# Full-width value operands, load-gated weights, a split spread and a new instruction order in a gated-recurrence + MLP kernel

## The chip, the cores and the metric

The kernel runs on one core of one Trainium2 chip. The metric is the time of one execution on the device in microseconds, from repeated runs; the median of three runs of the kernel before is 234.4 us (233.44 to 235.23).

The core has five engines with a queue of instructions each, worked off in order: TensorE (PE in the profile, with its weight loads shown apart as PEld), VectorE (DVE), ScalarE (ACT), GpSimd (POOL) and SyncE (SP). Here SP only issues transfers. An engine that waits holds up everything behind it in its own queue.

## What is computed

Two layers. The first is a gated linear recurrence per batch (4) and head (8), over 768 steps, with 48 features a head; the second is an MLP from 384 to 2048 and back, with a periodic activation.

```python
f = 1.0 / (1.0 + np.exp(-f_logit))
for t in range(S):
    state = f[:, :, t, :, None] * state + np.einsum('bhd,bhe->bhde', k[:, :, t], v[:, :, t])
    y[:, :, t] = np.einsum('bhd,bhde->bhe', q[:, :, t], state)
...
h = x @ w_in                    # x: y as (3072 tokens, 384)
s = np.sin(alpha * h)
g = h + s * s / (alpha + 1e-09)
out = g @ w_out
```

Inputs and output are float32 in HBM; the kernel computes its matmuls in bf16.

## The kernel before

**Tiling.** The 768 steps are cut into 6 chunks of 128. A *unit* u is one chunk and two of the four batches, so there are 12 units, and each has four loads of 384 KB (f, k, q, v; three buffers of each). Per unit, ScalarE computes the log gate (Exp, Ln), TensorE sums it over the steps with a triangular mask ("cs"), and ScalarE exponentiates the sums with both signs ("Gi" and "G"). k is multiplied by one and q by the other into a bf16 tile "qk", and v is copied into a bf16 tile "vb".

**Attend, per chunk and batch.** The 8 heads are handled as 4 pairs, head r * 4 + p standing in half r of pair p, 64 columns each of which 48 are used. k and q are transposed (on TensorE for the first four chunks, by transfers for the last two); scores "aps" are made per pair and half (64 rows of the array); VectorE multiplies them by the causal mask into "at", one tile for each half r; and the output "y" (128 rows of features, 4 pairs, 128 steps) is gathered in PSUM from the old state (`inter_`, L424, 128 x 128 stationary) and from the chunk itself (`intra_`, L437). In `intra_` the stationary operand is the 64 columns of one head's values, and the result goes to the 64 rows of half r, so TensorE works there with a 128*64 tile. In chunk 0 there is no state, and pair 1 is spread over three blocks at once from a second tile "v1". Last, `kv_` and `st_` make the new state.

**Spread.** y is copied to xT (bf16, features by tokens). The MLP needs 384 features in 3 blocks of 128; the three pairs p = 0, 2, 3 fill them with gaps of 16, and pair 1 is moved into the gaps by six small transfers (`spread`, L488), in every chunk but the first, where `intra_` writes there at once.

**MLP, per chunk.** For each of 16 feature blocks: 3 matmuls give h (512 tokens; in chunk 0 twice 256 tokens, a tile for each pair of batches), ScalarE takes the sine (L514), POOL, VectorE or ScalarE squares it (L522, L520), VectorE adds into g (L527); then 16 matmuls for each batch give the output o (L546), which is copied and stored. ScalarE's sine and its exponentials need different tables, so each change between them is a table load of about 1.3 us.

**The order.** The functions only describe operations: the engines an operation may run on with the cost on each, what it depends on, which buffers it takes. A list scheduler (`in_order`) simulates the five engines and emits the operation that can start earliest by these costs; ties go to the lower rank, and an operation with a choice of engines compares its start on each plus that engine's BIAS. Loads, h, cs and the ScalarE operations that use a table keep given orders (LOADS, PHASES). PSUM for the recurrence is a ring of three buffers "a", shared by cs, transposes, scores, y and kv. On the chip only the order on each engine and the real dependencies hold, not the planned times.

**Weights.** w_in comes in two halves of eight transfers, w_out in four, all issued by POOL. They depend on nothing. `W_AFTER` holds times (15, 22 and 52 us) before which the planner does not place them; it fixes their place in POOL's order and nothing else.

Of the kernel before, what the change touches and what calls it, by code (L numbers as in the profile page):

```python
# [51 lines left out]
LATENCY = {"PE": 260, "ACT": 120, "DVE": 120, "POOL": 150, "SP": 0}  # L52
# [76 lines left out]
def kernel(  # L129
# [20 lines left out]
    nc = tc.nc  # L150
# [55 lines left out]
    v1_b = [consts.tile([C, 2, 2, 3 * E], BF16, name=f"v1{i}") for i in range(2)]  # L206
    v_b = [consts.tile([C, 2, 2, HP, E], BF16, name=f"vb{i}") for i in range(NV)]
# [21 lines left out]
    for i in range(max(NQ, NV)):  # L229
        for ts in (lf_b, v_b, v1_b, qk_b):  # L230
            if i >= len(ts):
                continue
            if ts is v_b:
                nc.vector.memset(ts[i][:, :, :, 0:2, D:], 0.0)
                nc.vector.memset(ts[i][:, :, :, 2:4, 0:16], 0.0)
            elif ts is v1_b:
                nc.vector.memset(ts[i], 0.0)
            else:
                nc.vector.memset(ts[i].rearrange("c x y r e -> c (x y r) e")[:, :, D:], 0.0)
# [5 lines left out]
    def load(u, n, rank):  # L245
# [9 lines left out]
        load_order.append(o)  # L255
# [6 lines left out]
    al_r = consts.tile([P, FB], F32)  # L262
    w_in_dma, w_out_dma = {0: [], 1: []}, {}
# [10 lines left out]
    def w_out_load(rank):  # L274
        src = moe_w_out.rearrange("(fb p) m -> p fb m", p=P)
        for g4 in range(4):
            def emit(e, gs=slice(4 * g4, 4 * g4 + 4)):
                nc.gpsimd.dma_start(out=w_out_bf[:, gs, :], in_=src[:, gs, :])
            w_out_dma[g4] = op(rank + 0.1 * g4, {POOL: 780}, emit, dma=2500)
            w_out_dma[g4].after = W_AFTER[2]  # L280

# [18 lines left out]
    def pre(u, rank):  # L300
        fb_, kb_, qb_, vb_ = (bufs[n, u] for n in "fkqv")
# [10 lines left out]
        def values(e):  # L312
            vi = tl["v", u].rearrange("c (b r p) d -> c (b r) p d", r=2, p=HP)
            vo = v_b[bufs["vb", u].place % NV].rearrange("c b r p e -> c (b r) p e")
            nc.vector.tensor_copy(vo[:, :, 0:2, :D], vi[:, :, 0:2, :])
            nc.vector.tensor_copy(vo[:, :, 2:4, 16:], vi[:, :, 2:4, :])
            if u < NU:
                v1 = v1_b[u].rearrange("c b r x -> c (b r) x")
                nc.vector.tensor_copy(v1[:, :, D:D + 32], vi[:, :, 1, :32])
                nc.vector.tensor_copy(v1[:, :, 2 * E:2 * E + 16], vi[:, :, 1, 32:])  # L320

        x = op(rank, {ACT: 850}, exp_, deps=[fb_.ready], holds=[fb_], table=EXP)
        l = op(rank, {ACT: 850}, ln_, deps=[x], takes=[lf], holds=[fb_], table=EXP)
        act = [x, l]
        made["v", u] = op(rank + 2, {DVE: 1000 if u < NU else 950}, values, deps=[vb_.ready], takes=[vv], holds=[vb_])
        late = []
        for i in range(2):
# [34 lines left out]
            c_ = op(rank + i, {PE: 170 if last else 420}, cs_, deps=[l], takes=[cb], holds=[lf])  # L362
            c_.line = "cs"
            cs_order.append(c_)
            gi = op(rank, {ACT: 450}, Gi_, deps=[c_], takes=[Gib], holds=[cb], table=EXP)
            g = op(rank, {ACT: 450}, G_, deps=[c_], holds=[cb], table=EXP)
# [3 lines left out]
            made["kh", m] = op(rank + i, MULS, km, deps=[gi, kb_.ready], takes=[qkb], holds=[kb_, Gib])  # L370
            made["qh", m] = op(rank + i, {DVE: 600}, qm, deps=[g, qb_.ready], takes=[qkb], holds=[qb_, cb])
            if not last:
                made["gl", m] = op(rank + i, {DVE: 160}, gl_, deps=[g], takes=[glb], holds=[cb])
        return act, late

    def pres(us, rank):
        parts = [pre(u, r) for u, r in zip(us, rank)]
        for i in range(len(parts) + 1):
            act_order.extend(parts[i][0] if i < len(parts) else [])
            act_order.extend(parts[i - 1][1] if i else [])  # L380
# [257 lines left out]
```

## Time and profile before

| | |
|---|---|
| median of three runs | 234.4 us |
| the profiled execution | 234.14 us |
| its span, first to last instruction | 232.4 us |
| TensorE busy | 193.7 us (83%) |
| VectorE busy | 167.4 us (72%) |
| ScalarE busy | 149.0 us (64%) |
| POOL busy | 121.2 us (52%) |
| read from HBM, written | 25.17 MB, 4.72 MB |
| chain of waits that ended last | TensorE 49%, VectorE 13%, transfers 13%, SP's queue 7%, POOL 6% |

How to read it: a row of the timeline has the start in us, the length in us, the engine, the line of the kernel, the operation, the tile of the array for TensorE, output and inputs, and the count of instructions merged into the row; in square brackets stand the idle time before it and what ended that. TensorE's matmuls are pipelined, and the profile models their ends, so two rows may overlap and a busy time holds more than the array's own work. The row of forty digits cuts the span into slices of 5.8 us and gives the busy tenths of each. A row of a group (`L546 PE MATMUL ...`) gives count, busy us, mean ns, and the idle time just before its instructions.

### The profile page before, as it was taken

The numbers are of one execution on the slowest core, as the hardware profiler recorded it, in microseconds if no ns is written. First come the engines' busy times: TensorE is split into PE (matmuls) and PEld (weight loads), VectorE is DVE, ScalarE is ACT, GpSimd is POOL, SyncE is SP. The second block draws the span as 40 slices with busy tenths as digits, with TensorE's granted clock in tenths as the row PEclk, the third lists the DMA queues.
The fourth block names the chain that finished last, engine by engine and source line by source line (L and its number), as shares of the span: only waits on it lengthen the run. The fifth ranks groups of instructions, "written<-read, shape, count | busy, mean of one in ns | idle before, by whom it ended". The sixth has DMA issues, their size and how long they took to land.

```text
span 232.4 us, 4292 instructions
## 1 busy us (share of the span) xinstructions
PE 193.7 (83%) x1529; PEld 111.8 (48%) x1529; DVE 167.4 (72%) x319; ACT 149.0 (64%) x239; POOL 121.2 (52%) x148
## 2 busy tenths in 40 slices
PE   0441587787769999987999999999979999799993
PEld 0330464655546655543555545544535454355552
DVE  4533548997956998988788998986845987477631
ACT  4640178988939985489899557767757555365500
POOL 5560341674832757635735644555335467588810
PEclk9999999799999999999999999999999999999999
DMA  7999999986890799973999944700049101010011
GB/s 154 212 190 211 208 209 219 222 146 91 144 174 7 142 188 227 190 185 85 192 249 184 208 71 115 171 0 3 35 112 189 36 1 39 14 68 34 34 71 68
DMA packets 115125, 29.61 MB, mean 127 GB/s; under 512 B 108720, under 2 KB 114336, under 8 KB 115104
## 3 DMA queue, kind: packets, MB, share of 16 engines
q1 hardware_dynamic: 111936, 26.19, 55.8%
q0 software_dynamic: 3168, 3.16, 8.4%
q8 instruction: 12, 0.20, 0.4%
q14 instruction: 9, 0.07, 0.1%
HBM read 25.17 MB, written 4.72 MB: 129 GB/s over the span
## 4 chain that ended last, share of the span: by engine, by line
PE 49%; DVE 13%; DMA 13%; SPq 7%; POOL 6%; issue 5%; ACT 5%; POOLq 0%; ACTq 0%
PE h L509 19%; PE o L546 18%; DMA v<-in_v_dram 6%; PE y L437 6%; DVE g L527 5%; SPq L488 4%; SPq L251 4%; POOL s L522 3%; DVE at L419 3%; DMA w_out_bf<-in_moe_w_out_dram 3%; DMA xT<-xT 2%; POOL qk L358 2%; PE aps L416 2%; DMA w_in_bf<-in_moe_w_in_dram 2%; ACT Gi L349 1%
## 5 line engine op out<-in xcount | busy, mean ns | idle before, releaser
L522 POOL TENSOR_TENSOR s<-s 128x512 f32<-128x512 f32 (+1 forms) x94 | 87.8, 944 | 63.5 <-ACT s L514 51.3
L514 ACT ACTIVATE s<-h,al_p 128x512 f32<-128x512 f32 (+1 forms) x112 | 67.6, 626 | 43.4 <-PE h L509 40.6
L527 DVE SCALAR_TENSOR_TENSOR g<-s,al_r,h 128x512 bf16<-128x512 f32 (+1 forms) x112 | 72.4, 664 | 19.1 <-POOL s L522 18.4
L509 PE MATMUL h<-xT,w_in_bf 128*128 128x512 bf16 (+1 forms) x336 | 78.5, 355 | 6.8 <-DMA xT<-xT 3.6
L546 PE MATMUL o<-w_out_bf,g 128*128 128x384 bf16 x384 | 78.5, 327 | 2.8 <-DMA w_out_bf<-in_moe_w_out_dram 1.9
L509 PEld LDWEIGHTS <-w_in_bf 128*128 128x128 bf16 x336 | 31.8, 99 | 33.0 <-issue 6.5
L546 PEld LDWEIGHTS <-g 128*128 128x128 bf16 x384 | 34.4, 97 | 27.6 <-issue 3.1
L358 POOL TENSOR_TENSOR qk<-k,Gi 128x384 bf16<-128x384 f32 x19 | 19.0, 1017 | 33.8 <-ACT Gi L349 27.1
L419 DVE TENSOR_TENSOR at<-aps,mask 128x512 bf16<-128x512 f32 x48 | 31.7, 682 | 1.4 <-PE aps L416 1.4
L437 PE MATMUL y<-at,vb 128*64 128x128 bf16 x184 | 19.6, 233 | 6.3 <-DVE at L419 5.7
L358 DVE TENSOR_TENSOR qk<-q,cs 128x384 bf16<-128x384 f32 x24 | 12.9, 546 | 8.1 <-ACT cs L345 4.1
L437 PEld LDWEIGHTS <-vb 128*64 128x64 bf16 x184 | 12.2, 114 | 13.5 <-issue 9.6
L606 ACT ACT_TABLE_LOAD x13 | 16.7, 1283 | 0.2
L458 DVE TENSOR_TENSOR st<-kv,gl 128x512 bf16<-128x512 f32 x20 | 13.7, 685 | 4.0 <-PE kv L452 4.0
L444 ACT CAST xT<-y 128x512 bf16<-128x512 f32 (+1 forms) x12 | 6.7, 562 | 14.8 <-PE y L437 14.6
L416 PE MATMUL aps<-tr 64*128 64x128 bf16 x192 | 10.8, 225 | 6.3 <-DVE qk L358 5.6
L399 PE MATMUL tp<-ident,qk 128*128 128x128 bf16 x128 | 11.5, 236 | 4.4 <-DVE al_p L290 2.4
L349 ACT ACTIVATE Gi<-cs 128x384 f32<-128x384 f32 x24 | 11.7, 486 | 4.2 <-PE cs L336 2.7
L336 PE MATMUL cs<-lf,mask 128*128 128x384 bf16 x24 | 8.1, 355 | 7.3 <-ACT lf L309 6.5
L554 DVE COPY osb<-o 128x384 f32<-128x384 f32 x14 | 7.7, 555 | 7.7 <-PE o L546 6.7
L399 PEld LDWEIGHTS <-qk 128*128 128x128 bf16 x128 | 9.2, 106 | 6.7 <-POOL qk L358 4.2
L416 PEld LDWEIGHTS <-tr 64*128 64x128 bf16 x192 | 6.0, 96 | 12.4 <-DVE qk L358 6.6
(53 smaller groups left out, 164.4 us busy)
## 6 DMA issues: line engine op xcount, KB each, us to landing
f<-in_f_logit_dram SPq DMA_DIRECT2D x12, 384.0 KB, 5.6
k<-in_k_dram SPq DMA_DIRECT2D x12, 384.0 KB, 5.4
q<-in_q_dram SPq DMA_DIRECT2D x12, 384.0 KB, 5.8
v<-in_v_dram SPq DMA_DIRECT2D x12, 384.0 KB, 6.2
out_dram<-osb SPq DMA_DIRECT2D x24, 192.0 KB, 2.1
w_out_bf<-in_moe_w_out_dram POOLq DMA_DIRECT2D x4, 384.0 KB, 6.5
w_in_bf<-in_moe_w_in_dram POOLq DMA_DIRECT2D x8, 128.0 KB, 5.6
xT<-xT SPq DMA_DIRECT2D x30, 16.0 KB, 1.8
```

The source lines that it names most:

```text
L349: nc.scalar.activation(out=tl["Gi", m], in_=tl["cs", m][:, :H * D], func=Act.Exp)
L358: engine[e].tensor_mul(qk_b[bufs["qk", m].place % NQ][:, "kq".index(n), :, :, :D], tl[n, u][:, i * H:(i + 1) * H, :].rearrange("c (r p) d ...
L399: nc.tensor.transpose(tl[x, "tp"][:, j * HP + p, :], qk_b[qkb.place % NQ][:, j, p, :, :].rearrange("c r e -> c (r e)"), ident)
L416: nc.tensor.matmul(aps[r][:, p, :], t[halves[r], p, :], t[halves[r], HP + p, :], start=True, stop=True)
L419: nc.vector.tensor_mul(tl[x, "at", r], tl[x, "a"][r], mask4)
L437: nc.tensor.matmul(tl[x, "y"][halves[r], blk, :], v_, tl[x, "at", r][:, p, :], start=(first and p == 0), stop=True, skip_group_check=True)
L509: nc.tensor.matmul(h[:, :n], w_in_bf[:, kb, fs], xT[:, kb, ts], start=(kb == 0), stop=(kb == KB - 1))
L514: nc.scalar.activation(out=s[:, :n], in_=tl[x, "h"][:, :n], func=Act.Sin, scale=al_p[:, fb:fb + 1])
L522: engine[e].tensor_mul(s2[:, :n], s[:, :n], s[:, :n])
L527: nc.vector.scalar_tensor_tensor(tl["g", c, fb][:, ts], tl[x, "s2"][:, :n], al_r[:, fb:fb + 1], tl[x, "h"][:, :n], Alu.mult, Alu.add)
L546: nc.tensor.matmul(tl["o", c, t], tl["g", c, fb][:, t * P:(t + 1) * P], w_out_bf[:, fb, :], start=(fb == 0), stop=(fb == FB - 1))
L606: nc.scalar.preload_act_table_set(now)
```

## The change

1. **Full-width values.** The tile vb gets, behind each head's 64 columns, 64 columns of zeros, so that `intra_` can take 128 columns: values and zeros for half 0, zeros and values for half 1. Each matmul now writes all 128 rows of y and adds zeros in the other half. v1 is laid out in seven fields with zeros between for the same purpose. The tiles are cleared whole at the start.
2. **Weight transfers gated by loads.** Ahead of each half of w_in and of w_out stands a one-element copy on POOL from a loaded tile: the second, the seventh and the sixteenth load of the list. The weight transfers come behind it in POOL's order.
3. **Spread in two halves.** The six transfers become two operations of three, each of which may go to SP or to POOL.
4. **A new order.** Other load order, phases (5 groups of sines instead of 7), ranks, biases and costs, and a rank offset for each kind of operation in each chunk (KIND).

```diff
-SPARE = 25
-LOADS = [("f", 0), ("f", 1), ("k", 0), ("q", 0), ("v", 0), ("q", 1), ("v", 1), ("k", 1), ("f", 2), ("k", 3), ("q", 2), ("k", 2), ("k", 4), ("f", 3), ("f", 5), ("v", 3), ("v", 2), ("q", 4), ("q", 3), ("f", 4), ("k", 5), ("q", 5), ("k", 6), ("v", 4), ("q", 6), ("v", 5), ("v", 6), ("v", 7), ("k", 7), ("f", 7), ("f", 6), ("q", 8), ("q", 7), ("f", 8), ("v", 8), ("k", 8), ("f", 9), ("k", 9), ("q", 9), ("v", 9), ("f", 10), ("k", 10), ("q", 10), ("v", 10), ("f", 11), ("k", 11), ("q", 11), ("v", 11)]
-W_AFTER = [15000, 22000, 52000]
-LAG = [50, 24, 32, 29, 28, 94]
-ATT = [-32, 18, 8, 12, -4, 16]
-PHASES = [("pre", [0]), ("pre", [1]), ("sin", 6), ("pre", [2]), ("sin", 16), ("pre", [3]), ("sin", 9),
-          ("pre", [4, 5]), ("sin", 16), ("pre", [6, 7]), ("sin", 4), ("pre", [8, 9]), ("sin", 29), ("pre",
-          [10, 11]), ("sin", 32)]
-RANK = [-100, 150, -190, 19, 50, -161, -104, -88, -100, -12, -96, -264]
-MULS = {"POOL": 1180, "DVE": 1000}
-BIAS = {"ACT": 100, "DVE": 100, "POOL": -200}
+SPARE = 15
+LOADS = [("k", 0), ("f", 0), ("q", 0), ("v", 0), ("f", 1), ("v", 1), ("q", 1), ("k", 1), ("f", 3),
+    ("k", 3), ("f", 2), ("q", 3), ("q", 2), ("f", 5), ("v", 3), ("v", 2), ("k", 2), ("k", 4),
...
+W_GATE = [1, 6, 15]
+LAG = [389, 183, 51, 210, 208, 289]
+ATT = [150, -130, -181, 58, -47, 55]
+PHASES = [("pre", [0]), ("pre", [1]), ("sin", 16), ("pre", [2, 3]), ("sin", 15), ("pre", [4, 5]),
+    ("sin", 17), ("pre", [6, 7, 8]), ("sin", 18), ("pre", [9, 10, 11]), ("sin", 46)]
+RANK = [-6, 628, -691, -10, 175, 71, 8, 20, -437, -18, -103, -123]
+MULS = {"POOL": 1020, "DVE": 750}
+KIND = {"v": [147, 9, 46, 75, 127, -2],
+        "cs": [-145, -32, -204, -182, -55, -258],
...
+SPREAD = {"SP": 1800, "POOL": 1600}
+BIAS = {"ACT": 400, "DVE": 500, "POOL": 500, "SP": -1800}
...
-    v1_b = [consts.tile([C, 2, 2, 3 * E], BF16, name=f"v1{i}") for i in range(2)]
-    v_b = [consts.tile([C, 2, 2, HP, E], BF16, name=f"vb{i}") for i in range(NV)]
+    v1_b = [consts.tile([C, 2, 2, 7, E], BF16, name=f"v1{i}") for i in range(2)]
+    v_b = [consts.tile([C, HP, 2, 2, 2, E], BF16, name=f"vb{i}") for i in range(NV)]
...
-                nc.vector.memset(ts[i][:, :, :, 0:2, D:], 0.0)
-                nc.vector.memset(ts[i][:, :, :, 2:4, 0:16], 0.0)
+                nc.vector.memset(ts[i], 0.0)
...
+    def weights_after(i, rank):
+        u, n = LOADS[W_GATE[i]][1], LOADS[W_GATE[i]][0]
+        return op(rank, {POOL: 100}, lambda e: nc.gpsimd.tensor_copy(seen[:, i:i + 1], tl[n, u][0:1, 0, 0:1]),
+                  deps=[bufs[n, u].ready], holds=[bufs[n, u]])
+
     def w_in_load(hf, rank):
+        gate = weights_after(hf, rank)
...
-                w_in_dma[hf].append(o := op(rank, {POOL: 550}, emit, dma=830 if n == E else 620 if n == D else 210))
-                o.after = W_AFTER[hf]
+                w_in_dma[hf].append(op(rank, {POOL: 550}, emit, deps=[gate],
+                                       dma=830 if n == E else 620 if n == D else 210))
...
-            vo = v_b[bufs["vb", u].place % NV].rearrange("c b r p e -> c (b r) p e")
-            nc.vector.tensor_copy(vo[:, :, 0:2, :D], vi[:, :, 0:2, :])
-            nc.vector.tensor_copy(vo[:, :, 2:4, 16:], vi[:, :, 2:4, :])
+            vo = v_b[bufs["vb", u].place % NV].rearrange("c p b r x e -> c p (b r) x e")
+            nc.vector.tensor_copy(vo[:, 0:2, :, 0, :D], vi[:, 0:2])
+            nc.vector.tensor_copy(vo[:, 2:4, :, 0, 16:], vi[:, 2:4])
...
                 if first and p == 1:
-                    v1 = v1_b[u][:, i, r, :]
-                    vs = ((0, v1[:, 0:E]), (2, v1[:, E:2 * E]), (1, v1[:, 2 * E:]))
+                    v1 = v1_b[u][:, i, r].rearrange("c x e -> c (x e)")
+                    vs = [(blk, v1[:, (2 * n + 1 - r) * E:(2 * n + 3 - r) * E]) for n, blk in enumerate((0, 2, 1))]
                 else:
-                    vs = ((POS[p], v_b[vb.place % NV][:, i, r, p, :]),)
+                    vs = [(POS[p], v_b[vb.place % NV][:, p, i].rearrange("c r x e -> c (r x e)")[:, r * E:(r + 2) * E])]
                 for blk, v_ in vs:
-                    nc.tensor.matmul(tl[x, "y"][halves[r], blk, :], v_, tl[x, "at", r][:, p, :],
-                                     start=(first and p == 0), stop=True, skip_group_check=True)
+                    nc.tensor.matmul(tl[x, "y"][:, blk, :], v_, tl[x, "at", r][:, p, :],
+                                     start=(first and p == r == 0), stop=(r == 1), skip_group_check=True)
...
-        def emit(e):
+        def emit(e, r):
             xT = tl["xT", c]
-            for r in range(2):
-                for blk, dst, src in ((0, D, 0), (2, 0, 16), (1, 0, 32)):
-                    engine[e].dma_start(out=xT[r * E + dst:r * E + dst + 16, blk, :],
-                                        in_=xT[r * E + src:r * E + src + 16, 3, :])
-        made["x", c] = op(rank, {SP: 3000}, emit, deps=[made["y", c, b] for b in range(B)],
-                          holds=[bufs["xT", c]], dma=300)
+            for blk, dst, src in ((0, D, 0), (2, 0, 16), (1, 0, 32)):
+                engine[e].dma_start(out=xT[r * E + dst:r * E + dst + 16, blk, :],
+                                    in_=xT[r * E + src:r * E + src + 16, 3, :])
+        made["x", c] = [op(rank, SPREAD, lambda e, r=r: emit(e, r), deps=[made["y", c, b] for b in range(B)],
+                           holds=[bufs["xT", c]], dma=150) for r in range(2)]
...
-        t = op(rank, {POOL: 700 if half else 1040, ACT: 420 if half else 630, DVE: 350 if half else 620}, sq, deps=[s], takes=[s2b], holds=[sb])
+        t = op(rank + KIND["sq"][c], {POOL: 640 if half else 1040, ACT: 420 if half else 640, DVE: 520 if half else 917}, sq, deps=[s], takes=[s2b], holds=[sb])
```

More of the change, by code (lines that the diff above doesn't have):

```diff
@@ L49, in __init__ @@
         self.line = table and "table"
-LATENCY = {"PE": 260, "ACT": 120, "DVE": 120, "POOL": 150, "SP": 0}
+LATENCY = {"PE": 260, "ACT": 160, "DVE": 180, "POOL": 180, "SP": 0}
 TABLE_LOAD, DMA_LATENCY, DMA_AHEAD = 1280, 1400, 1000
@@ L278, in emit @@
                 nc.gpsimd.dma_start(out=w_out_bf[:, gs, :], in_=src[:, gs, :])
-            w_out_dma[g4] = op(rank + 0.1 * g4, {POOL: 780}, emit, dma=2500)
-            w_out_dma[g4].after = W_AFTER[2]
+            w_out_dma[g4] = op(rank + 0.1 * g4, {POOL: 780}, emit, deps=[gate], dma=2500)
     def alpha(rank):
@@ L465, in attend @@
+            tr = op(rank + KIND["tr"][c], {DVE: 640, ACT: 970}, tr_, deps=[qt], takes=[trb], holds=[tpb])
         else:
             tr = op(rank, {SP: 1300}, tr_, deps=[made["kh", m], made["qh", m]], takes=[trb], holds=[qkb], dma=3000)
-        a = op(rank, {PE: 450}, a_, deps=[tr], takes=ab + atb, holds=[trb])
-        ms = [op(rank, {DVE: 690}, lambda e, r=r: m_(e, r), deps=[a], holds=[ab[r], atb[r]]) for r in range(2)]
+        a = op(rank + KIND["a"][c], {PE: 400}, a_, deps=[tr], takes=ab + atb, holds=[trb])
@@ L528, in add @@
                                            tl[x, "h"][:, :n], Alu.mult, Alu.add)
-        a = op(rank, {PE: 330 if half else 645}, mm, deps=needs, takes=[hb], holds=[bufs["xT", c]])
+        a = op(rank + KIND["h"][c], {PE: 340 if half else 655}, mm, deps=needs, takes=[hb], holds=[bufs["xT", c]])
         a.line = "h"
@@ L533, in first @@
         h_order.append(a)
-        s = op(rank, {ACT: 470 if half else 600}, sin_, deps=[a, made["al"]], takes=[sb], holds=[hb], table=TRIG)
-        t = op(rank, {POOL: 700 if half else 1040, ACT: 420 if half else 630, DVE: 350 if half else 620}, sq, deps=[s], takes=[s2b], holds=[sb])
-        made["g", c, fb, ts.start] = op(rank, {DVE: 410 if half else 690}, add, deps=[t], takes=[gb], holds=[s2b, hb])
+        s = op(rank, {ACT: 455 if half else 645}, sin_, deps=[a, made["al"]], takes=[sb], holds=[hb], table=TRIG)
+        t = op(rank + KIND["sq"][c], {POOL: 640 if half else 1040, ACT: 420 if half else 640, DVE: 520 if half else 917}, sq, deps=[s], takes=[s2b], holds=[sb])
+        made["g", c, fb, ts.start] = op(rank + KIND["g"][c], {DVE: 420 if half else 685}, add, deps=[t], takes=[gb], holds=[s2b, hb])
         return s
@@ L557, in store @@
             nc.sync.dma_start(out=out[t * S + c * C:t * S + (c + 1) * C, :], in_=tl["osb", c, t])
-        v_ = op(rank, {DVE: 550, ACT: 650}, ev, deps=[prev], takes=[sbuf], holds=[ob])
+        v_ = op(rank + KIND["ev"][c], {DVE: 520, ACT: 500}, ev, deps=[prev], takes=[sbuf], holds=[ob])
         op(rank, {SP: 500}, store, deps=[v_], holds=[sbuf], dma=700)
@@ L566 @@
     made["al"] = alpha(EARLY)
+    for u in range(NCH * NU):
+        for n in "fkqv":
+            load(u, n, EARLY)
+    load_order += [bufs[x].ready for x in LOADS]
     w_in_load(0, EARLY)
```

103 lines of the change are left out of this document (56 added, 47 removed), and 4 rows, old and new, of the table LOADS.

## The prediction

> **What bounds the kernel now.** I read the forty slices of the page first, then the stretches, then TensorE's instructions in order of time, then the waits.
>
> ```profile
> span 232.4 us, 4292 instructions
> PE   0441587787769999987999999999979999799993
> DVE  4533548997956998988788998986845987477631
> DMA  7999999986890799973999944700049101010011
> GB/s 154 212 190 211 208 209 219 222 146 91 144 174 7 142 188 227 190 185 85 192 249 184 208 71 115 171 0 3 35 112 189 36 1 39 14 68 34 34 71 68
> 0.00:72.00 72.00, 43.29 (x421) 30.97 (x422) 46.61 (x117) 44.41 (x77) 34.13 (x64) 0.98 0.99 176
> 72.00:220.00 148.00, 142.03 (x1062) 76.10 (x1061) 117.42 (x197) 103.54 (x162) 85.41 (x83) 1.00 0.52 109
> ```
>
> The stretch rows give, after the length, the busy us of PE, PEld, DVE, ACT and POOL, then clock, DMA share and GB/s. There are two regimes. From 72 to 220 us TensorE is busy 142.03 of 148: what shortens its work there shortens the kernel, as long as VectorE (117.42, four fifths of the stretch) follows. Up to 72 us TensorE is busy 43.29 of 72 and waits for others, while the DMA slices stand at 9 tenths for some 46 us. The profiled execution took 234.14 us, 1.7 more than its span and next to the median of 234.4; I work from 234.1.
>
> **Part 1, the padded values.** A TensorE busy time contains the modelled end of each matmul, so I measure from start to start.
>
> ```profile
> 182.96 0.82 PE L509 MATMUL h<-xT,w_in_bf 128*128 128x512 bf16 x3
> 183.62 0.39 PE L424 MATMUL y<-tr,st 128*128 128x128 bf16 x4
> 183.84 0.33 PE L546 MATMUL o<-w_out_bf,g 128*128 128x384 bf16 x1
> ...
> 187.24 0.81 PE L509 MATMUL h<-xT,w_in_bf 128*128 128x512 bf16 x3
> 187.98 0.41 PE L437 MATMUL y<-at,vb 128*64 128x128 bf16 x4
> 188.32 0.50 PE L546 MATMUL o<-w_out_bf,g 128*128 128x384 bf16 x2
> ...
> 55.89 0.42 PE L437 MATMUL y<-at,vb 128*64 128x128 bf16 x8
> 56.24 0.39 PE L450 MATMUL kv<-st,ident 128*128 128x512 bf16 x1
> ...
> 72.00:220.00 148.00, 12.96 (x132) 7.89 (x130) 1.00 0.52 109
> ```
>
> L424 is what the padded matmul will be: the whole array as stationary, 128 columns moving. Three h matmuls before it take 183.62 - 182.96 = 0.66 us and its four take 183.84 - 183.62 = 0.22. The same three h matmuls before an intra-chunk block take 187.98 - 187.24 = 0.74, and the four 64-wide matmuls 188.32 - 187.98 = 0.34. Nobody is waiting there: entering and leaving the half-width tile costs 0.08 + 0.12 = 0.20 us a block, and the padded form has no such border. The last row, the stretch view of L437 alone, counts 132 of them after 72 us: 33 blocks of four. Where both halves stand together the eight take 56.24 - 55.89 = 0.35 us, and in the padded form 2 x 0.22 = 0.44: with the border of 0.08 saved, nothing is won. One such pair lies after 72 us, so 31 blocks win 31 x 0.20 = 6.2. A block with the aps matmuls (64*128, a border of its own) right behind it keeps one border, so I take **-6.0**; ends 0 (something else is as late as TensorE) and 33 x 0.20 = -6.6.
>
> The blocks before 72 us are not counted here, because TensorE waits there anyway. The zero halves add to the output rows of the other half; the one group start per tile and the masks stay, so no instruction is added: eight per attend as before, twelve in chunk 0.
>
> The row speaks against a rule of the Trainium skill here. TensorEngine Tiling, Overview, expects up to twice the speed from a 64-wide stationary, since independent tiles run at the same time; by it padding throws half the array away, and the sum would lose its first term. Rows 55.89 and 56.24 show some of that overlap, in the one order where the halves meet; it returns below as a rival.
>
> **Part 2, the head.**
>
> ```profile
> 4.44 0.84 ACT L306 ACTIVATE f<-f 128x768 f32<-128x768 f32 x1 [2.35 <-DMA f<-in_f_logit_dram]
> 9.16 4.27 POOL L269 DMA_DIRECT2D w_in_bf<-in_moe_w_in_dram  x8
> 9.67 13.18 DMA v<-in_v_dram
> 12.24 1.01 ACT L407 COPY tr<-tp 128x1024 bf16<-128x1024 bf16 x1 [1.90 <-PE tp L399]
> 18.68 0.55 DVE L358 TENSOR_TENSOR qk<-q,cs 128x384 bf16<-128x384 f32 x1 [4.00 <-DMA q<-in_q_dram]
> 19.83 0.60 PE L416 MATMUL aps<-tr 64*128 64x128 bf16 x7 [0.25 <-DVE qk L358]
> 22.87 0.36 DVE L315 CAST vb<-v 128x384 bf16<-128x384 f32 x1 [2.50 <-DMA v<-in_v_dram]
> 23.66 1.28 DVE L419 TENSOR_TENSOR at<-aps,mask 128x512 bf16<-128x512 f32 x2
> 25.82 0.48 ACT L444 CAST xT<-y 128x384 bf16<-128x384 f32 x1 [10.77 <-PE y L437]
> 29.07 3.03 PE L509 MATMUL h<-xT,w_in_bf 128*128 128x256 bf16 x15 [0.57 <-ACT xT L444]
> 30.33 1.33 ACT L514 ACTIVATE s<-h,al_p 128x256 f32<-128x256 f32 x3
> 53.04 1.61 POOL L278 DMA_DIRECT2D w_out_bf<-in_moe_w_out_dram  x2
> ...
> f<-in_f_logit_dram SPq DMA_DIRECT2D x12, 384.0 KB, 5.6
> ```
>
> Both batches of unit 0 have their transposes by 12.24 + 1.01 = 13.25, and the first mask product starts at 23.66. Two things hold it: the score tiles come free only when unit 1's q has landed (18.68; three "a" buffers, two of them under unit 1's cumulative sums), and VectorE stands in its order at unit 1's values until 22.87. Both loads are late because the first weights went out at 9.16, as POOL was idle; the planner had put them behind 15 us. The gates make the order real: the weights start when f of unit 0 has landed, and the planner knows it. RANK 628 also puts unit 1 behind unit 0.
>
> New head: f of unit 0 is now second on the queue. The first load was there at 4.44; at the page's rate near 200 GB/s the 384 KB before it cost 2.0 us more. So transposes at 15.3, then scores 0.6, and from mask to y copy 25.82 + 0.48 - 23.66 = 2.6, the second batch again about 2.7 behind it: h starts near 21.2 instead of 29.07. The gated weights, issued from about 6.5 on for 4.3 us, are 2.7 us ahead of before, so they do not hold it. The first sine follows the sums of unit 1 and a table load: about 22.5 against 30.33, **8 us** earlier. How much of that reaches 72 us is not in the trace: the later loads cannot all move (DMA is at 9 tenths to 46 us), yet the slices from 46 to 75 us (8, 6, 8, 9, 0) hold idle DMA, and the w_out weights, issued now from 53.04 on, come with the sixteenth load. Ends 0 and -8; nearer the far end, since most waits in the head are for order and not for bytes: **-5.0**.
>
> What the gates cost: three one-element copies on POOL. Behind them POOL's own queue holds the weight issues (4.27 us for eight), the k products and the squares; for those the sines wait, then TensorE. If the gate is reached after its load has landed it costs its own 0.1 us; the slower rival below is the other end.
>
> **Part 3, the spread.**
>
> ```profile
> 194.53 0.70 DVE xT L444
> 195.25 4.25 SPq L488 DMA_DIRECT2D xT<-xT  x6
> 198.92 1.78 DMA xT<-xT
> 200.74 0.60 PE h L509 x2
> ...
> L509 PE MATMUL h<-xT,w_in_bf 128*128 128x512 bf16 x240 | 63.3, 379 | 3.7 <-DMA xT<-xT 3.6
> ```
>
> Six issues hold SP for 4.25 us, and h waits for the last landing. With three of them on POOL the last would go out three issues, about 1.8 us, earlier. But SP has a bias of -1800 and a half costs 1800: in the planner's key the second half on SP ties with its real time, while POOL carries +500. So I expect POOL to get a half only where loads fill SP's queue. All spreads together make TensorE wait 3.6 us: between 0 and -3.6, I take **-0.5**. The Trainium skill's DMA: Bandwidth & Descriptors, Issuing engines are not separate DMA queues, calls the saved issue time usually small beside the transfer; here 4.25 us of issue stand against 1.78 of transfer, so the rows would give more than the page, if POOL were used.
>
> **What costs nothing.**
>
> ```profile
> L234 DVE MEMSET vb<- 128x64 uint32 x4 | 0.4, 112 | 0.0
> L237 DVE MEMSET v<- 128x384 uint32 x2 | 0.8, 378 | 0.1
> L606 ACT ACT_TABLE_LOAD x13 | 16.7, 1283 | 0.2
> 8.24 1.39 DVE L358 TENSOR_TENSOR qk<-k,Gi 128x384 bf16<-128x384 f32 x1 [0.17 <-ACT Gi L349]
> ```
>
> Whole tiles are cleared now: (378 - 112) / 320 = 0.83 ns an element gives 0.9 us for each of four (1024 words) and 0.8 for each of two (896 words), 5.2 in all against 8 x 0.11 + 2 x 0.38 = 1.6. VectorE then starts 3.6 us later, near 7; its first product stood at 8.24 and now comes 2 us later, so the wait for the loads covers it (uncovered: +3.6 at most). The value copies keep their elements. Seven sine phases become five, so 9 table loads stand against 13: 4 x 1.28 = 5.1 us of ScalarE, an engine that is not last. The new order in the TensorE stretch could win the few us that it idles (148 - 142.03 = 6.0, the 3.6 of the spreads among them) or lose as much: 0, ends -2.4 and +6.
>
> **Sum:** 234.1 - 6.0 - 5.0 - 0.5 = **222.6 us**. With its unknowns 215 to 228.
>
> **Rivals.** (a) *The head's gain is eaten before 72 us.* From 35 to 64 us VectorE's slices stand at 7 to 9 while chunk 0's tiles go through, so work that starts earlier may only queue there; against it, TensorE's own idle of 28.7 us in that stretch. 234.1 - 6.5 = 227.6, about 228. (b) *VectorE takes over TensorE's place.* It would have to do the 117.4 us in 148 - 6 = 142, 83%, with the waits of a fixed order on top; if all of Part 1 turns into such waits and the head is eaten too: about 233.5, no change. For it: slices of 9 in both rows; against: VectorE idles in the same slices in which TensorE is full. (c) *The halves do overlap.* If the block pairs ran mostly as in row 55.89, padding would cost 2 x 0.22 - 0.35 = 0.09 for each of 20 attends, so +1.8 for Part 1: 234.1 + 1.8 - 5.5 = 230.4. Against it, 31 of 33 blocks stand alone. This is the page's rule on tiles. (d) *Slower: POOL stands at its gates.*
>
> ```profile
> DMA to landing us min/median/max: 5.0/6.2/13.2
> L522 POOL TENSOR_TENSOR s<-s 128x512 f32<-128x512 f32 x70 | 73.6, 1057 | 43.7 <-ACT s L514 39.8 <-DVE g L527 2.9 <-DVE at L419 0.4
> ```
>
> A v load needs 6.2 us in the middle and up to 13.2. POOL does most of the squares, and with three s buffers its stop becomes everybody's. If the second and third gate each come a landing too early, halfway between these at 9.7 us, 19.4 are added: 222.6 + 19.4 = 242. It decides from about 14 us of stops in sum on. Against it: the planner knew the load's time, and its costs (7 loads of 2.1, twelve weight pieces for 8.3, 2.8 of start and latency) put the seventh load behind twelve pieces at 25.8 us, where it really landed at 22.87: gates should open early rather than late.
>
> **Chances.** Forecast 0.62; (a) 0.14; (b) 0.09; (c) 0.05; (d) 0.10. Within 1% of 234.4 (231.9 to 236.7, about what three runs spread: 233.44 to 235.23) counts as no change: (b), 0.09. Faster: 0.62 + 0.14 + 0.05 = 0.81. Slower: 0.10. Range: down to 213, if the head passes whole (-3) and the spreads and the order give their rest (-6); up to 233, which takes in (a), (c) and half of (b). Left out is (d), some of (b) and a little below: under 0.2.
>
> **What will show it.** Part 1: matmuls of line y in shape 128*128, four of them 0.22 us apart from the next block, h before them 0.66; a TensorE stretch with 6 us less. If the four still take 0.34, or if more time between h blocks ends at VectorE, Part 1 was wrong. Part 2: the first mask product near 16 and the first h near 21 us, no wait for unit 1's v in front of it; the start of the full TensorE slices near 65 instead of 72. Part 3: SP issues six in a row as before. Slower rival: POOL idle for loads at the gate copies, ScalarE's sines waiting behind. The forecast is wrong above 228 or below 215.

## The result and the profile after

The changed kernel takes 221.6 us (median of four runs, 220.9 to 222.4) against 233.9 us for the kernel before: a ratio of 0.947, 95% interval 0.941 to 0.952. In a second session it took 221.3 us against 234.1 (0.943, 0.936 to 0.950). The forecast was 222.6 us, so the total is right. The sections below show that most of its terms were not. Medians below count every execution of a kernel; ratios and intervals leave out those that stand more than 1.5% above its fastest.

First the page of the changed kernel, and its two stretches in the columns of the prediction (length, busy us of PE, PEld, DVE, ACT and POOL, clock, DMA share, GB/s).

```profile
span 219.3 us, 4322 instructions
PE   0259754687999898977799999999999999999993
DVE  7578768569887999895589898568878858778700
PEclk9999999669999999999699999999999999999998
DMA  7999999999991999989599998555510101101111
```
```profile
0.00:72.00 72.00, 48.21 (x474) 35.14 (x475) 54.05 (x121) 50.02 (x91) 36.51 (x70) 0.95 1.13 176
72.00:220.00 148.00, 138.19 (x1057) 79.27 (x1055) 111.12 (x181) 115.08 (x185) 63.00 (x65) 0.98 0.60 115
```

TensorE has done 474 matmuls by 72 us where it had done 421, 4.9 us more of busy time (a part of it slower matmuls, at a clock of 0.95 for 0.98), and what is left ends at 219.3 instead of 232.4. POOL has lost 21.7 us of work (121.2 to 99.5): it does 29 squares fewer, 25 of which went to ScalarE. ScalarE gains 16 us, though it loads four tables fewer. The clock row has two slices of 6 from 38 to 49 us and one near 107; the row of before has a single 7.

The head of the changed kernel, in order of time:

```profile
7.15 0.17 POOL L287 COPY seen<-f 1x1 f32<-1x1 f32 x1 [3.05 <-DMA f<-in_f_logit_dram]
7.27 4.04 POOL L295 DMA_DIRECT2D w_in_bf<-in_moe_w_in_dram  x8
16.91 2.57 DVE L440 TENSOR_TENSOR at<-aps,mask 128x512 bf16<-128x512 f32 x4
21.62 0.17 POOL L287 COPY seen<-q 1x1 f32<-1x1 f32 x1 [9.29 <-DMA q<-in_q_dram]
21.66 2.59 PE L529 MATMUL h<-xT,w_in_bf 128*128 128x256 bf16 x15
24.63 1.57 ACT L534 ACTIVATE s<-h,al_p 128x256 f32<-128x256 f32 x4
```

Mask products from 16.91 us on (23.66 before), the first h at 21.66 (29.07), the first sine at 24.63 (30.33). The second gate holds POOL for 9.29 us, with nothing urgent behind it.

The padded blocks, first beside full-width neighbours, then with the scores behind them, then both halves together:

```profile
53.79 0.39 PE L445 MATMUL y<-tr,st 128*128 128x128 bf16 x4
54.01 0.39 PE L458 MATMUL y<-at,vb 128*128 128x128 bf16 x4
54.24 0.82 PE L529 MATMUL h<-xT,w_in_bf 128*128 128x256 bf16 x6
...
116.04 0.39 PE L458 MATMUL y<-at,vb 128*128 128x128 bf16 x4
116.36 0.40 PE L437 MATMUL aps<-tr 64*128 64x128 bf16 x8
...
118.72 0.61 PE L458 MATMUL y<-at,vb 128*128 128x128 bf16 x8
119.16 1.46 PE L529 MATMUL h<-xT,w_in_bf 128*128 128x512 bf16 x6
```

From start to start: 0.22 and 0.23 us, like the state's own block in front of it, where it was 0.34; 0.32 ahead of the scores, whose border stays; 0.44 for eight.

### The profile page after: what moved, and what is told of

It reads as the page before. It is cut to its first block, busy times and chain, and to the rows that moved or that the text cites. A ratio compares the mean times of both kernels' runs of the same rounds, so it can differ in the third digit from the quotient of the medians.

```text
span 219.3 us, 4322 instructions
## 1 busy us (share of the span) xinstructions
PE 186.4 (85%) x1529; PEld 114.4 (52%) x1529; DVE 165.2 (75%) x301; ACT 165.1 (75%) x275; POOL 99.5 (45%) x134
## 4 chain that ended last, share of the span: by engine, by line
PE 54%; DMA 13%; ACT 10%; DVE 8%; issue 5%; SPq 5%; POOL 4%; POOLq 0%; ACTq 0%; DVEq 0%
PE o L566 24%; PE h L529 20%; DMA q<-in_q_dram 7%; SPq L271 5%; DMA w_out_bf<-in_moe_w_out_dram 4%; PE y L458 3%; DVE g L547 3%; DMA w_in_bf<-in_moe_w_in_dram 3%; ACT f L333 3%; POOL s L542 2%; PE aps L437 2%; ACT Gi L376 2%; ACT L628 2%; POOL w_in_bf L295 2%; PE y L445 1%
## 5 line engine op out<-in xcount | busy, mean ns | idle before, releaser
L542 POOL TENSOR_TENSOR s<-s 128x512 f32<-128x512 f32 (+1 forms) x65 | 58.5, 911 | 69.6 <-ACT s L534 58.0
L566 PEld LDWEIGHTS <-g 128*128 128x128 bf16 x384 | 36.5, 98 | 25.3 <-issue 1.5
L385 POOL TENSOR_TENSOR qk<-k,Gi 128x384 bf16<-128x384 f32 x22 | 21.6, 1002 | 17.8 <-ACT Gi L376 17.7
L540 ACT ACTIVATE s<-s 128x512 f32<-128x512 f32 (+1 forms) x36 | 20.8, 584 | 0.9
L363 PE MATMUL cs<-lf,mask 128*128 128x384 bf16 x24 | 8.8, 375 | 12.6 <-ACT lf L336 10.3
L458 PE MATMUL y<-at,vb 128*128 128x128 bf16 x184 | 18.5, 228 | 0.5 <-DVE at L440 0.5
L333 ACT ACTIVATE f<-f 128x768 f32<-128x768 f32 x12 | 10.0, 836 | 6.5 <-POOL seen L287 5.3
L458 PEld LDWEIGHTS <-vb 128*128 128x128 bf16 x184 | 13.1, 102 | 2.4 <-issue 0.2
L574 ACT COPY osb<-o 128x384 f32<-128x384 f32 x16 | 7.7, 479 | 8.8 <-PE o L566 8.6
L465 ACT CAST xT<-y 128x512 bf16<-128x512 f32 (+1 forms) x20 | 11.2, 567 | 1.0 <-PE y L458 0.8
```

The lines of the kernel that those rows point to most:

```text
L333: nc.scalar.activation(out=tl["f", u], in_=tl["f", u], func=Act.Exp, scale=-1.0)
L385: engine[e].tensor_mul(qk_b[bufs["qk", m].place % NQ][:, "kq".index(n), :, :, :D], tl[n, u][:, i * H:(i + 1) * H, :].rearrange("c (r p) d ...
L458: nc.tensor.matmul(tl[x, "y"][:, blk, :], v_, tl[x, "at", r][:, p, :], start=(first and p == r == 0), stop=(r == 1), skip_group_check=True)
L540: nc.scalar.activation(out=s2[:, :n], in_=s[:, :n], func=Act.Square)
L542: engine[e].tensor_mul(s2[:, :n], s[:, :n], s[:, :n])
L566: nc.tensor.matmul(tl["o", c, t], tl["g", c, fb][:, t * P:(t + 1) * P], w_out_bf[:, fb, :], start=(fb == 0), stop=(fb == FB - 1))
```

## The experiments

Each was run beside the kernel before; the ratio is to it, with its 95% interval.

| kernel | median us | ratio |
|---|---|---|
| changed kernel, second session | 221.3 | 0.943 (0.936 to 0.950) |
| before + padded values | 230.1 | 0.984 (0.977 to 0.991) |
| before + one gate | 234.2 | 1.002 (0.997 to 1.006) |
| before + split spread | 234.0 | 0.998 (0.994 to 1.001) |
| changed order alone | 230.5 | 0.985 (0.979 to 0.991) |
| changed, half-width values | 226.8 | 0.967 (0.959 to 0.974) |
| changed, no gates | 224.5 | 0.962 (0.954 to 0.969) |
| changed, spread on SP alone | 226.8 | 0.966 (0.959 to 0.973) |
| changed, all second halves on POOL | 222.9 | 0.950 (0.942 to 0.958) |
| changed, f of unit 0 first | 222.0 | 0.945 (0.942 to 0.948) |
| changed, second gate on v | 219.8 | 0.935 (0.930 to 0.940) |
| changed, filler matmuls | 222.9 | 0.947 (0.939 to 0.954) |

All of them keep the order of the kernel that they start from; only what an operation emits is edited. They were run in three more sessions, each on a chip of its own, where the kernel before had medians of 234.3 us (order alone, padded values, half-width values, no gates), 234.1 (second session, one gate, spread on SP, all halves on POOL) and 235.0 (the rest); a difference of a microsecond between kernels of different sessions means little.

### The padded values in the old order

The tiles, the clearing, the copies, `intra_` and `kv_` of the change, put into the kernel before:

```diff
...
-                    vs = ((POS[p], v_b[vb.place % NV][:, i, r, p, :]),)
+                    vs = [(POS[p], v_b[vb.place % NV][:, p, i].rearrange("c r x e -> c (r x e)")[:, r * E:(r + 2) * E])]
...
-                    nc.tensor.matmul(tl[x, "y"][halves[r], blk, :], v_, tl[x, "at", r][:, p, :],
+                    nc.tensor.matmul(tl[x, "y"][:, blk, :], v_, tl[x, "at", r][:, p, :],
```

> The kernel before, in its own order, with nothing changed but the padded values (tiles, clearing, copies, intra-chunk and state matmuls). Theory (borders of the half-width tile cost TensorE 0.20 us a block, 31 blocks after 72 us): 6.0 us faster than before, near 228, blocks of four y matmuls 0.22 us long. Rival (the waits behind the elementwise engines eat it): within 1.5 us of before, 233. Rival (the halves overlapped, padding doubles the work): 1 to 2 us slower than before, 236.

Measured: 230.1 us, ratio 0.984, so 2 to 5 us faster (4 by the medians) and not 6. Blocks of its TensorE timeline, two beside full-width neighbours and one ahead of the scores (L436 is the y block, L508 h, L545 o, L415 the scores):

```profile
180.82 0.81 PE L508 MATMUL h<-xT,w_in_bf 128*128 128x512 bf16 x3
181.47 0.39 PE L436 MATMUL y<-at,vb 128*128 128x128 bf16 x4
181.69 0.65 PE L545 MATMUL o<-w_out_bf,g 128*128 128x384 bf16 x3
182.18 0.39 PE L436 MATMUL y<-at,vb 128*128 128x128 bf16 x4
182.50 0.40 PE L415 MATMUL aps<-tr 64*128 64x128 bf16 x8
```

h ahead of the block takes 0.65 us and the block 0.22: the borders are gone as reckoned. Added up over all blocks after 72 us, the start-to-start times of the two traces differ by 5.7 us. The gain is smaller, and waits took a part of its place. TensorE's waits on VectorE's additions, in the waits of before and then of this run (time in all, times, longest):

```profile
PE h L509 <- DVE g L527: 2.3, 5, 0.9
```
```profile
PE h L508 <- DVE g L526: 3.7, 8, 0.9
```

They grow by 1.4 us, 1.2 of them after 72 us; but TensorE's listed waits of all kinds grow there by 0.7 only, from 6.3 to 7.0, and in the head, where `at` is waited for longer (8.4 us for 5.7) and qk shorter (1.7 for 5.6), they change places. So listed waits account for 0.7 us of the 1.7 that lie between 5.7 and the measured 4; where the rest went stays open. It is not the clock: executions at 0.993 differ by 3.9 us (233.7 and 229.8 on average). Overlap of the halves as the stronger effect is ruled out: that kernel would have been slower.

### Half-width values in the new order

```diff
...
-                    vs = [(POS[p], v_b[vb.place % NV][:, p, i].rearrange("c r x e -> c (r x e)")[:, r * E:(r + 2) * E])]
+                    vs = [(POS[p], v_b[vb.place % NV][:, p, i, r, 0, :])]
...
-                    nc.tensor.matmul(tl[x, "y"][:, blk, :], v_, tl[x, "at", r][:, p, :],
-                                     start=(first and p == r == 0), stop=(r == 1), skip_group_check=True)
+                    nc.tensor.matmul(tl[x, "y"][halves[r], blk, :], v_, tl[x, "at", r][:, p, :],
+                                     start=(first and p == 0), stop=True, skip_group_check=True)
```

> The changed kernel in its own order, with the intra-chunk matmuls back on the 64 columns of one head and on half the rows of y; the padded tiles stay as they are. Theory of the borders: the same 6 us are lost, near 227.5. After 72 us more blocks of the changed order may have both halves together (8 in a row), which lose nothing: each such pair takes 0.4 us off the loss. Rival (the new order alone makes the gain): within 1.5 us of 221.6.

Measured: 226.8 us, 5.5 more than the changed kernel. The runs of this kernel were granted different clocks, 0.948 to 0.977. At 0.977, which all four runs of the changed kernel had in the second session (220.7 to 222.4 us), it took 225.1 in one execution: about 3.7 us more. The borders alone come to less here: after 72 us the changed kernel has 16 blocks of four and 8 pairs of eight, and a pair takes 0.45 us padded against 0.36 half-width, so that the start-to-start times of the changed kernel and of the new order alone (next section) differ by 2.9 us in sum, where the old order had 5.7. The padding is thus worth 3 to 4 us in the new order and about 4 in the old one; what the medians show beyond that goes with the lower clock.

### The new order alone

The three edits together: half-width `intra_`, no gate copies, all spread transfers on SP.

> The changed kernel's order with all three other parts undone: half-width intra-chunk matmuls, no gate copies (the weight transfers go out as soon as POOL reaches them), all spread transfers on SP. Theory (6 for the values, 5 for the head, of which the gates are a part, 0.5 to 2 for the spread): 228 to 231, so 3 to 6 us under the kernel before. If the parts are worth nothing beside the order: 222. If the order needs its parts: 234 or above.

Measured: 230.5 us, ratio 0.985, inside the theory's 228 to 231. The order alone is worth 2 to 5 us (3.8 by the medians); the three parts together take the other 9.2 (230.5 to 221.3). Its four executions were granted 0.970, those of the changed kernel 0.977.

### No gates in the new order

```diff
-        return op(rank, {POOL: 100}, lambda e: nc.gpsimd.tensor_copy(seen[:, i:i + 1], tl[n, u][0:1, 0, 0:1]),
+        return op(rank, {POOL: 100}, lambda e: None,
```

> The changed kernel in its own order without the three gate copies: the weight transfers depend on nothing and go out as soon as POOL reaches them, so the first half near 4.1 us instead of 7.3, the second right behind it instead of 21.9. Theory (the early weights delay the loads of units 0 and 1, as in the kernel before): first h matmul 3 to 5 us later than 21.7, 2 to 4 us slower in all, 224 to 226. Rival (the gates only move the same bytes about, POOL gets free 9 us earlier): within 1 us of 221.6, or 1 us faster, since h waits for the second half of w_in near 30 us in the changed kernel.

Measured: 224.5 us, 3.2 more than the changed kernel. The head, in order of time:

```profile
4.00 4.08 POOL L295 DMA_DIRECT2D w_in_bf<-in_moe_w_in_dram  x8
10.92 4.09 POOL L295 DMA_DIRECT2D w_in_bf<-in_moe_w_in_dram  x8
25.52 1.92 PE L529 MATMUL h<-xT,w_in_bf 128*128 128x256 bf16 x15
```

Both halves of w_in leave before 15.1 us, and the first h starts at 25.52 instead of 21.66. Of these 3.9 us the spans of the two profiles keep 1.7 at the end (221.0 and 219.3); the medians differ by 3.2. The theory holds in the new order, with 2 to 3 us.

### One gate in the old order

```diff
...
                 def emit(e, j=j, p0=p0, r0=r0, n=n, r=r):
+                    if hf == j == p0 == r == 0:
+                        nc.gpsimd.tensor_copy(seen, tl["v", 1][0:1, 0, 0:1])
```

> The kernel before in its own order, with one gate: POOL copies one element of unit 1's v (seventh load) ahead of the first weight transfer, so the weights start when that load has landed. Theory (the early weights delayed the loads of unit 1, for which the order stands): v of unit 1 lands near 17 instead of 22.9 us, the first mask product starts near 18 instead of 23.7, the first h near 25 (now held by the weights), 4 us earlier than before, and 2 to 3 us of it reach the end: 231 to 232. Rival (the head's gain is eaten by the weights that come later): first h not before 28, 234.

Measured: 234.2 us, ratio 1.002: nothing won. The head, in order of time:

```profile
17.55 0.37 POOL L271 COPY seen<-v 1x1 f32<-1x1 f32 x1 [6.97 <-DMA v<-in_v_dram]
18.30 1.28 DVE L422 TENSOR_TENSOR at<-aps,mask 128x512 bf16<-128x512 f32 x2
23.71 0.37 PE L512 MATMUL h<-xT,w_in_bf 128*128 128x256 bf16 x1 [0.57 <-ACT xT L447]
26.03 0.37 PE L512 MATMUL h<-xT,w_in_bf 128*128 128x256 bf16 x1 [1.94 <-DMA w_in_bf<-in_moe_w_in_dram]
27.08 2.96 PE L512 MATMUL h<-xT,w_in_bf 128*128 128x256 bf16 x13 [0.68 <-DMA w_in_bf<-in_moe_w_in_dram]
36.15 0.94 PE L512 MATMUL h<-xT,w_in_bf 128*128 128x256 bf16 x7 [1.22 <-DMA w_in_bf<-in_moe_w_in_dram]
40.55 0.40 PE L419 MATMUL aps<-tr 64*128 64x128 bf16 x7 [1.35 <-DVE qk L361]
```

Mask products at 18.30 instead of 23.66, as the mechanism said: the early weights had held unit 1's loads, and those the whole head. But h then waits for its weights piece by piece, so the 5.4 us have become 2.0 where h gets going (27.08 for 29.07), and 0.8 at the scores of 40.55 us, which started at 41.37 before. By 48 us that is gone too: an addition into g that started at 47.66 starts at 48.10. In this execution the clock was half from 40.9 to 47.7 us, before from 41.9 to 45.3, but executions at an equal clock, 0.993, show no gain either (233.5 to 234.5 us, before 232.5 to 234.3). The same bytes had to come, and the old order made nothing of the earlier start.

### The spread

All transfers of the changed kernel's spreads on SP, and the second half of all five on POOL:

```diff
-                engine[e].dma_start(out=xT[r * E + dst:r * E + dst + 16, blk, :],
+                nc.sync.dma_start(out=xT[r * E + dst:r * E + dst + 16, blk, :],
```
```diff
-                engine[e].dma_start(out=xT[r * E + dst:r * E + dst + 16, blk, :],
+                (nc.gpsimd if r else nc.sync).dma_start(out=xT[r * E + dst:r * E + dst + 16, blk, :],
```

> The changed kernel in its own order, with the three spread halves that it sends by POOL put on SP at the same place. Theory (a half on POOL saves three SP issues of 0.6 us in each of three chunks, but only where TensorE waits for the landing, which it does for 1.6 us in all at the start of a chunk): 0 to 3 us slower. If the split is worth nothing: within 0.7 us.

> The changed kernel in its own order, with the second half of all five spreads on POOL, the two of chunks 4 and 5 too. Theory: in chunks 4 and 5 TensorE no longer stands idle at the spread (other matmuls fill it), so nothing is won: within 0.7 us. Rival (each serial spread costs its 1.8 us as in the kernel before): 2 to 3 us faster.

Measured: 226.8 us on SP alone, 5.4 above the changed kernel; 222.9 with all five split, no gain (the intervals overlap). The issues of the changed kernel (first session), and the waits in which TensorE stands for xT, first in the changed kernel (second session) and then with SP alone:

```profile
L508 SPq DMA_DIRECT2D xT<-xT x21: 512/587/1360, 67.4 to 178.4; - x21
L508 POOL DMA_DIRECT2D xT<-xT x9: 484/534/687, 68.0 to 128.5; - x9
```
```profile
PE h L529 <- DMA xT<-xT: 1.1, 2, 0.7
```
```profile
PE h L529 <- DMA xT<-xT: 5.5, 3, 2.6
```

POOL issues nine transfers, three halves, up to 128.5 us: chunks 1 to 3. Without them TensorE's wait grows from 1.1 to 5.5 us (1.6 in the first session), about what the medians lose. All of it stands in two chunks: 2.6 us in chunk 1 and 2.9 in chunk 2, none in chunk 3. The two profiles lie 7.1 us apart at the end, but 3.4 of that had come before the first spread, where this execution had the half clock from 31 us on; the other 3.7 come at the spreads of chunks 1 and 2, and nothing is added later. In chunks 4 and 5 SP sends all six one after another, and TensorE does not wait; there POOL wins nothing.

The same split in the kernel before:

> The kernel before in its own order, with the second half of each of its five spreads on POOL at the same place. In its trace TensorE waits 3.6 us in all for spreads. Theory (a split saves up to three SP issues where TensorE waits, and nothing where other matmuls fill the time): 1.5 to 3.6 us faster, 231 to 232.5. Rival (POOL standing at its half delays the squares behind it, whose order was not planned for that): no change or slower.

Measured: 234.0 us, ratio 0.998. TensorE's wait for xT fell from 3.6 to 2.7 us only, and it moved. The spread of chunk 1 and the h that waits for it, then all waits:

```profile
72.25 1.85 SPq L488 DMA_DIRECT2D xT<-xT  x3
74.49 1.56 POOL L488 DMA_DIRECT2D xT<-xT  x3
78.77 1.24 PE L509 MATMUL h<-xT,w_in_bf 128*128 128x512 bf16 x4 [0.95 <-DMA xT<-xT]
```
```profile
PE h L509 <- DMA xT<-xT: 2.7, 3, 1.2
```

In chunks 4 and 5 the theory holds: 3.0 us of waiting are gone. In chunks 1 and 2 POOL, which has k products to do first, comes to its half 2.2 and 2.1 us after SP has begun, later than SP alone would have issued the fourth transfer (three take 1.85 us), and there the wait grows from 0.6 to 2.7 us. So gain and loss nearly cancel. POOL's own standing at its halves (1.2 us in chunk 3, 1.8 in chunk 4), on which the rival was built, falls where TensorE does not wait for xT.

So the split is worth about 5 us in an order made for it. In the old one it pays only where POOL is free in time, and nothing that can be measured in all.

### Three tries at the head

The first two loads exchanged:

```diff
+            n = {("k", 0): "f", ("f", 0): "k"}.get((n, u), n)
```

> The changed kernel in its own order, with the first two loads exchanged: f of unit 0 first, k second. f lands 2 us earlier, the first weights start 2 us earlier as well. If an earlier head passes to the end as the later head of the run without gates did (3.9 us at the first h, 2 to 3 us at the end): 1 us faster, 220.5. Rival (the loads set the pace of the head, the bytes are the same): within 0.7 us of 221.5.

Measured: 222.0 us, no change. The head, and then the same copy of v in the changed kernel's second session:

```profile
5.05 4.04 POOL L296 DMA_DIRECT2D w_in_bf<-in_moe_w_in_dram  x8
14.82 0.36 DVE L343 CAST vb<-v 128x384 bf16<-128x384 f32 x1 [4.90 <-DMA v<-in_v_dram]
24.28 2.25 PE L530 MATMUL h<-xT,w_in_bf 128*128 128x256 bf16 x15
```
```profile
11.61 0.80 DVE L342 CAST vb<-v 128x384 bf16<-128x384 f32 x1 [0.38 <-DMA v<-in_v_dram]
```

The first weights, gated by f, went out 2 us earlier too, at 5.05, close behind the issue of unit 0's v (4.62). That v landed 3.2 us later than in the changed kernel, VectorE stood 4.9 us for it, and the first h came at 24.28 instead of 21.51, the first sine at 27.2 instead of 24.5. ScalarE did not wait for unit 1's f.

The second gate on v of unit 1, one load earlier:

```diff
-        return op(rank, {POOL: 100}, lambda e: nc.gpsimd.tensor_copy(seen[:, i:i + 1], tl[n, u][0:1, 0, 0:1]),
+        return op(rank, {POOL: 100}, lambda e: nc.gpsimd.tensor_copy(seen[:, i:i + 1], tl[("v", 1) if i == 1 else (n, u)][0:1, 0, 0:1]),
```

> The changed kernel in its own order, with the second gate on v of unit 1 (sixth load) instead of q of unit 1 (seventh). The second half of w_in, for which h waits 2 us near 30 us, is issued some 2 to 4 us earlier, and the loads behind it come later. Theory (the wait for w_in near 30 us costs the end its length): 1 to 2 us faster. Rival (the bytes only change places): within 0.7 us of 221.5.

Measured: 219.8 us, ratio 0.935 (0.930 to 0.940): 1.5 us under the changed kernel's 221.3, with intervals that overlap a little (0.936 to 0.950), and the fastest median of the study. Three of its executions took 219.5 to 220.1 us; the fourth took 1022.4, and why is not known. Its h matmuls, and those of the changed kernel's second session, where they wait for the second half of w_in:

```profile
19.45 4.16 POOL L295 DMA_DIRECT2D w_in_bf<-in_moe_w_in_dram  x8
29.75 0.61 PE L529 MATMUL h<-xT,w_in_bf 128*128 128x256 bf16 x4 [0.29 <-DMA w_in_bf<-in_moe_w_in_dram]
31.20 1.15 PE L529 MATMUL h<-xT,w_in_bf 128*128 128x256 bf16 x9
```
```profile
21.84 4.11 POOL L295 DMA_DIRECT2D w_in_bf<-in_moe_w_in_dram  x8
29.64 0.27 PE L529 MATMUL h<-xT,w_in_bf 128*128 128x256 bf16 x1 [0.41 <-DMA w_in_bf<-in_moe_w_in_dram]
31.37 0.61 PE L529 MATMUL h<-xT,w_in_bf 128*128 128x256 bf16 x4 [1.46 <-DMA w_in_bf<-in_moe_w_in_dram]
```

The weights leave 2.4 us earlier, h of that block starts at 29.75 instead of 31.37, and of this lead of 1.6 us the spans keep 1.1 (217.8 and 218.9). A gain is likely, but not clear of the noise between sessions.

Matmuls of constants in TensorE's wait near 36 us, which compute nothing that is used:

```diff
+            if c == 0 and b == 3:
+                for _ in range(48):
+                    nc.tensor.matmul(aps[0][:, 0, :], ident, mask, start=True, stop=True)
```

> The changed kernel with 48 matmuls of constants (128 columns) ahead of the scores of chunk 0, batch 3, into a score tile that is overwritten: they add work that nobody uses, 2.7 us at the full clock, in TensorE's wait near 35 to 38 us. If the half clock that the trace shows from 36 to 48 us follows from that wait: the granted clock there rises to 1.0 and the kernel is 1 to 2 us faster. If the clock falls for another reason: no change, or up to 2 us slower where the 48 outlast the wait.

Measured: 222.9 us, ratio 0.947, no change. TensorE alone in two stretches of the changed kernel (first session), then with the filler (length, PE busy, clock, DMA share, GB/s):

```profile
28.00:36.00 8.00, 5.35 (x52) 1.00 1.25 204
36.00:48.00 12.00, 7.21 (x65) 0.72 1.35 187
```
```profile
28.00:36.00 8.00, 6.98 (x48) 0.57 1.25 200
36.00:48.00 12.00, 8.44 (x119) 1.00 1.19 182
```

The half clock moved: in this run it came from 28 to 35 us, before the filler, which ran from 36.63 us on. So the question that the filler was to decide was not put, and what lowers the clock here stays open.

## Why the prediction was right, and where it was not

**Part 1, the padded values (-6.0).** The mechanism was right to the hundredth: 0.22 for 0.34 us, h at 0.65 for 0.74, 0.45 for a pair, and a border kept ahead of the scores. The term of the sum was too large: it measured 4 us in the old order (2 to 5), where the borders come to 5.7 (30 blocks of four and a pair, since the window's count takes in a block that begins at 71.83 us). Waits took 0.7 us of the difference, so rival (b) has a small share at most; the rest is open. In the new order the term had to be smaller still: the forecast took the old order's one pair in 32, and the new one has 8 in 24, which brings the borders to 2.9 us. Rival (c) is excluded as the stronger effect; in those pairs it is what padding costs.

**Part 2, the head (-5.0).** The chain was right: mask products at 16.91 (near 16 forecast), first h at 21.66 (21.2), the first sine at 24.63 (22.5, 2 us too early). One sign did not come: TensorE's slices stand at 8 and 9 from 55 us on, but at 7 from 93 to 110 us, so the full stretch begins near 110 and not near 65. What failed is the step that put the 5 us down to the gates and the earlier start: "most waits in the head are for order and not for bytes". The gate in the old order brought the mask products 5.4 us forward and the end not at all; rival (a) is what happens there, with weights in the place of the elementwise engines. (Its argument against, 28.7 us of idle TensorE, belongs to the first 72 us; from 35 to 64 us TensorE idles 6.3.) In the new order the gates are worth 2 to 3 us. Whatever else the new order wins in the head, no run separates.

**Part 3, the spread (-0.5).** Wrong, by 5 us. The step that failed is "SP has a bias of -1800 and a half costs 1800", from which POOL was to get a half only where loads fill SP's queue. The planner gave POOL a half in three of five chunks. Why, no run shows; in the trace loads do not hold SP there: its last load ahead of the first spread is issued by 62.95 us, and the spread starts at 66.87 (second session). The bound of 3.6 us was the second error: it was the old order's wait, and the serial spread costs more in the new one. In chunk 2 of the kernel before, ten o matmuls stand between SP's first issue (105.44 us) and the h that waits (110.39); with SP alone in the new order there is one (99.76 to 103.47). The rows' verdict on issue time against transfer time, six issues of 0.59 us against 1.8 for a landing, was the right reading; the Trainium skill's sentence in DMA: Bandwidth & Descriptors, Issuing engines are not separate DMA queues, that the saving is usually small beside the transfer, does not describe this place.

**The order (0, ends -2.4 and +6).** Alone it gives 3.8 us by the medians (2 to 5), beyond the near bound of 2.4. That bound was taken from TensorE's idle time after 72 us only, and so left out what an order can win in the head.

**The sum.** The forecast of 222.6 stood on 6.0 + 5.0 + 0.5 + 0. The runs put the order at about 4 and the other parts at 9 together, taken back together (230.5 to 221.3). Taken back one at a time they cost 5.5, 3.2 and 5.4 by the medians, which is 14.1; executions at 0.977 alone give 3.7, 2.2 and 5.3, about 11, from one or two executions each. Whether the parts overlap is not clear of the noise. That the total was right is luck: too much for the values and the head stood against too little for the spread and the order. Rival (d) did not come: the second gate held POOL for 9.29 us, but before the first sine, when POOL had no squares to do.

## What to carry to other kernels

Measure a short matmul from its neighbour's start to the next one's start: a few half-width matmuls among full-width ones cost two borders that their own row does not show, and padding with zeros can be cheaper. An edit that frees time is worth what the order behind it can use: gates and a split spread gave 2 to 3 and 5 us in an order planned with them, while a gate and the same split gave nothing in the old one, the split because POOL came too late to half of its transfers. So such edits are to be costed, and tested, together with the order. A bound taken from a wait holds only for the order in which that wait was seen.

## What the hardware showed that was not expected

The granted TensorE clock is part of the result here. The kernel before ran at 0.993 in its profile, the changed kernel at 0.973, with 0.72 from 36 to 48 us where the kernel before had 0.86; a kernel whose program differs only after 60 us (the spread on SP alone) had 0.69 already from 28 to 36 us and 0.954 over the span, in one execution, and 0.977 in another. At equal clock, 0.977, that kernel took 226.6 us against 220.7 to 222.4, so the spread's cost is not the clock's; but differences of one or two microseconds between such kernels should be compared at equal clock.
